# A long convolution by a two-step Fourier transform: the layout of the spectrum between step one and step two

## The chip, the cores and the metric

One core of a Trainium2 chip runs the whole kernel. The metric is device time in microseconds, the median of the runs made; lower is better. The core has a matrix engine (TensorE, in the profile PE for matmuls and PEld for weight loads), VectorE (DVE), ScalarE (ACT), GpSimd (POOL) and SyncE (SP), which issues most DMAs.

## The reference: what is computed

A block with two branches, all in float32, on 2048 tokens by 640 channels. The first branch is a long causal convolution by channel (an H3 mixer), gated by the normalized input; the second a token-mixing MLP. Cut to what matters here:

```python
h = layernorm(x) * (1 + ca) + sa                  # ca, sa, ga from silu(c) @ w_mod
kv = short_conv4(k, shift_k) * v                  # four taps, causal, by channel
y = irfft(rfft(pad(kv)) * rfft(pad(ssm_k)))[:S]   # by channel, length 2 S = 4096
x = x + ga * h * (y + kv * ssm_D)
x = x + gb * mlp_over_tokens(layernorm(x) * (1 + cb) + sb)
```

The change lies in the transform `rfft` of `kv` and of `ssm_k`.

## The kernel before, in words

The five blocks of 128 channels are handled one after another (`c` = 0 to 4, the loop at L510). A block's transform is done on TensorE with float32 matmuls. Time is written as 64 by 32, time = 32 n1 + n2, frequency as 64 k1 by 32 k2.

**Step one** (`step1(side, t)`, L210 to L222) sums over n1. `side` 0 is `kv`, from the tile X, whose channel pairs are read as weights with a step of 32 words; `side` 1 is the filter `ssm_k`, brought into order by `perm` in the tile P and read as contiguous weights. One call takes eight channel pairs (`a` = 0 to 7, pair i = 8 t + a); four calls make a side. For each pair two matmuls, of the cosines and of the sines (`ri`), write 128 columns each, the 64 values of k1 for either channel half, to 64 partitions of a PSUM tile of 1024 words. The columns of one matmul lie side by side; even pairs go to the tile's first bank and odd ones to the second. One ScalarE instruction (L220) then copies the 1024 words to the spectrum Z in SBUF. It reads PSUM in order and writes words at a step of two, so that two neighbouring pairs stand side by side for each k1.

**Step two** (`f2(g)`, L224 to L252) sums over n2. A group g has eight values of k1; for each of them, for the real and the imaginary part and for both channel halves h, a matmul with 64 columns reads all 64 channel columns of its k1 from Z (32 of each side). In Z they lie as 32 pairs of words, 256 words apart. The two halves write different partitions of PSUM. The product of both spectra follows: ScalarE copies the filter's part (L238, tile kt), VectorE multiplies twice (`mul`, L243 and L245, tile p), and POOL, or VectorE for the last group, adds or subtracts into Y (`add`, L251). Every operation of this kind stands in the profile under L59, where the helper TT is.

**The inverse** is `i2` (L263, from Y; ScalarE's copies at L271 write T2, which shares its place with side one of Z) and `i1` (L282, which reads T2 as pairs of words 128 words apart). `gate` multiplies and adds the result into the residual x.

The order of the work is written by hand. For a block c above 0: eight groups of step two, with VectorE's short convolution for the next block (`kv_ops`, its results go to X) mixed in by `dv`; then step one of side 0 for the next block, t = 0 and 1; `i2(0)`; step one t = 2; `i2(1)`; t = 3; `i1(0)`; step one of side 1, t = 0; `i1(1)`; t = 1 to 3. So step two of a block follows the copy of its last tile of side 1. PSUM tiles are taken in turn from a ring of three (`psum`, L69), so a tile of step two can be written again once the VectorE products of the group three before it have read it. In block 4 the fill is layer statistics (`x1s`, L509) and there is no next step one; a few matmuls for the modulation (`mod_part`, L342) stand in its place. After the five blocks come the second norm and the token MLP (L432, L1026, and L951 with seven products in place of eight), which the change doesn't touch.

Constants come ready from the host: F1 (the cosines and sines of step one, 128 columns each, made by `_constants` from `f1`), W2 for step two, V1 and V2 for the inverse.

Of the kernel before, what the change touches and what calls it, by code (L numbers as in the profile page):

```python
# [11 lines left out]
AF = mybir.ActivationFunctionType  # L12
# [8 lines left out]
def _constants():  # L21


    n1, n2, k1, k2 = np.arange(64), np.arange(32), np.arange(64), np.arange(32)
    a = 2 * np.pi * ((1 + 4 * k1)[None, :] * n1[:, None] % 256) / 256
    f1 = np.zeros((2, 64, 2, 2, 64))
    for h in range(2):
        f1[h, :, 0, h], f1[h, :, 1, h] = np.cos(a), np.sin(a)
    ang = 2 * np.pi * ((1 + 4 * k1)[None, :, None] * n2[:, None, None] / 8192
                       + (k2[None, None, :] * n2[:, None, None] % 32) / 32)  # L30
    w2 = np.zeros((2, 32, 2, 64, 2, 2, 32))
    for c in range(2):
        w2[0, :, c, :, 0, c] = np.cos(ang)
        w2[1, :, c, :, 0, c] = -np.sin(ang)
        w2[0, :, c, :, 1, c] = np.sin(ang)
        w2[1, :, c, :, 1, c] = np.cos(ang)
    ang = 2 * np.pi * (k2[:, None] * n2[None, :] % 32) / 32
    c, s = np.cos(ang), np.sin(ang)
    v2 = np.tile(np.concatenate([c, -s, s, c], 1), (4, 1))
    ang = 2 * np.pi * ((1 + 4 * k1)[:, None, None] * (32 * n1[None, None, :] + n2[None, :, None]) % 8192) / 8192  # L40
    v1 = np.tile(np.stack([np.cos(ang), np.sin(ang)], 1).reshape(64, 4096) / 2048, (2, 1))
    sel = np.zeros((128, 128))
    sel[0, 0:64] = sel[1, 64:128] = 1
    small = np.concatenate([f1.reshape(128, 256), v2, np.eye(128)[:, 0:36], sel], 1)
    return {"small": small.astype(np.float32), "w2": w2.reshape(128, 8192).astype(np.float32),
            "v1": v1.astype(np.float32)}
# [3 lines left out]
def mixer_kernel(ctx: ExitStack, tc: tile.TileContext, q, k, v, shift_k, ssm_k, ssm_D, w1, b1, w2, b2, c,  # L50
# [7 lines left out]
    act, dve, pool, pe, sync = nc.scalar, nc.vector, nc.gpsimd, nc.tensor, nc.sync  # L58
# [3 lines left out]
    def mem(tag, n, name=None):  # L62

        return sb.tile([128, n], F32, name=name or tag, tag=tag, bufs=1)
# [4 lines left out]
    def psum(slot=None):  # L69

        uid[0] += 1
        slot = ring[uid[0] % len(ring)] if slot is None else slot
        return psp.tile([128, 1024], F32, name=f"pst_{uid[0]}", tag=f"pst{slot}", bufs=1)
# [6 lines left out]
    T_z, T_y, T_v1 = mem("z", 8192), mem("y", 4096), mem("v", 4520)  # L80
# [11 lines left out]
    KT = [T_kt[:, 512 * i:512 * i + 512] for i in range(2)]  # L92
    TV = T_kt[:, 1024:1536].rearrange("p (n i) -> p n i", i=64)

    Z = T_z.rearrange("p (s t a k e) -> p s t a k e", s=2, t=4, a=8, e=2)
    T2 = T_z[:, 4096:8192].rearrange("p (a m e) -> p a m e", a=32, e=2)
    Y = T_y.rearrange("p (r i k) -> p r i k", r=2, i=32)
    W2 = [t.rearrange("p (k m) -> p k m", m=64) for t in T_w2]
# [2 lines left out]
    F1, V2, ID = SM[:, 0:256], SM[:, 256:384], SM[:, 384:420]  # L101
# [108 lines left out]
    def step1(side, t, later=False):  # L210

        ps = psum()
        for a in range(8):
            i = 8 * t + a
            lhs = KSP[:, i] if side else X.rearrange("p (m i) -> p i m", i=32)[:, i]
            o = 512 * (a % 2) + 128 * (a // 2)
            for ri in range(2):
                pe.matmul(ps[64 * ri:64 * ri + 64, o:o + 128], lhs, F1[:, 128 * ri:128 * ri + 128], start=True,  # L218
                          stop=True)
        evac = lambda: act.activation(Z[:, side, t].rearrange("p a k e -> p e a k"),  # L220
                                      ps.rearrange("p (e a k) -> p e a k", a=8, e=2), AF.Copy)
        return evac if later else evac()  # L222

    def f2(g):  # L224

        ps = psum()
        for kk in range(8):
            k1 = 8 * g + kk
            for ri in range(2):
                for h in range(2):  # L230
                    o = 128 * kk + 64 * ri
                    rhs = bass.AP(tensor=T_z.tensor, offset=T_z.offset + 128 * h + 2 * k1,
                                  ap=[T_z.ap[0], [256, 32], [1, 2]])
                    pe.matmul(ps[64 * h:64 * h + 64, o:o + 64], W2[k1 // 32][:, 2 * (k1 % 32) + ri], rhs, start=True, stop=True)  # L234
        pv = ps.rearrange("p (m s i) -> p m s i", s=2, i=32)
        xs_ = pv[:, :, 0]
        kt = KT[g % 2]
        act.activation(kt.rearrange("p (m i) -> p m i", i=32), pv[:, :, 1], AF.Copy)  # L238
        pa, pb = P[:, 1024 * (g % 2):1024 * (g % 2) + 512], P[:, 1024 * (g % 2) + 512:1024 * (g % 2) + 1024]
        m16 = lambda t: t.rearrange("p (m i) -> p m i", i=32)  # L240

        def mul():
            TT(dve, m16(pa), xs_, m16(kt), ALU.mult)  # L243
            sw = bass.AP(tensor=kt.tensor, offset=kt.offset + 32, ap=[kt.ap[0], [64, 8], [-32, 2], [1, 32]])
            TT(dve, pb.rearrange("p (k r i) -> p k r i", k=8, r=2), xs_.rearrange("p (k r) i -> p k r i", r=2), sw,  # L245
               ALU.mult)

        def add(eng=pool):
            for ri, t, op in ((0, pa, ALU.subtract), (1, pb, ALU.add)):
                t = t.rearrange("p (k r i) -> p r k i", k=8, r=2)  # L250
                TT(eng, Y[:, ri, :, 8 * g:8 * g + 8].rearrange("p i k -> p k i"), t[:, 0], t[:, 1], op)  # L251
        return mul, add  # L252
# [20 lines left out]
    def i1(half, slot=None):  # L273

        ps = psum(slot)
        for jj in range(8):
            for ri in range(2):
                for e in range(2):
                    p = slice(64 * e, 64 * e + 64)
                    for b in range(2):  # L280
                        n2 = 16 * b + 8 * half + jj
                        pe.matmul(ps[64 * b:64 * b + 64, 512 * e + 64 * jj:512 * e + 64 * jj + 64],  # L282
                                  V1[p, ri, n2], T2[p, :, 32 * ri + n2], start=ri == 0, stop=ri == 1)
        return ps
# [200 lines left out]
    for t in range(4):  # L485
        step1(0, t)
# [3 lines left out]
    for t in range(4):  # L490
        step1(1, t)
# [18 lines left out]
    for c in range(NC):  # L510
# [3 lines left out]
        for g in range(8):  # L514
            m_, a_ = f2(g)
            if pend_m:
                pend_m()
            if pend_a:
                pend_a()
            pend_a, pend_m = (pend_m and pa_next), m_  # L520
            pa_next = a_
            if c:
                for f_ in ac[2 * g:2 * g + 2]:
                    f_()
            if cn is None and g < 4:

                act.activation(X[:, 512 * g:512 * g + 1], epsc, AF.Copy)
                for b in range(2):
                    sync.dma_start(X[64 * b:64 * b + 64, 512 * g:512 * g + 512],
                                   dram(w1, (16 * b + g) * F, [[32 * F, 64], [1, 512]]))  # L530
            dv(-(-len(fill) // max((6 if c else 8) - g, 1)))
            if c and cn is not None and g == 3:
                perm_add(cn)
# [13 lines left out]
        if c == 0:  # L547
            mod_load(0, 4, P[:, 0:1920])
            for t in range(4):
                step1(0, t)  # L550
            ps = psum()
# [45 lines left out]
        else:  # L597
# [6 lines left out]
            t = mem("in", 4288, "wb3")  # L604
# [4 lines left out]
        if c:  # L609
            dv(7 if cn is not None else 8)  # L610
            i2(0)
            if cn is None:
                mod_part(tap, 3, pl[3])
                i2(1, dve)
                t = mem("y", 4096, "wb2")
# [19 lines left out]
        for half in range(2):  # L635
            ps = i1(half)
# [37 lines left out]
    start = []  # L674
# [84 lines left out]
    ps = i1(1, s1)  # L759
# [121 lines left out]
    for f_ in range(4, NF):  # L881
        ps = psum().rearrange("p (h m) -> p h m", h=2)
# [123 lines left out]
    for s in range(NW):  # L1006
# [15 lines left out]
        for f_ in range(NF):  # L1022
            u = U[f_]
            for k, (w, r) in enumerate(((wh, 0), (wh, 2), (wl, 0))):
                for h in range(2):
                    pe.matmul(acc[s][:, h, 0:320], w[:, f_].bitcast(F32R), u[r + h].bitcast(F32R),  # L1026
                              start=f_ == 0 and k == 0, stop=f_ == NF - 1 and k == 2)
# [29 lines left out]
def build(inputs):  # L1057
    import concourse.bacc as bacc

    nc = bacc.Bacc("TRN2", target_bir_lowering=False, num_devices=1)  # L1060
    arrays, args = {}, []

    def add(name, a):
        a = np.ascontiguousarray(a)
        arrays[f"in_{name}_dram"] = a
        args.append(nc.dram_tensor(f"in_{name}_dram", a.shape, mybir.dt.from_np(a.dtype), kind="ExternalInput").ap())

    for name in _INS:
        a = np.asarray(inputs[name])
        add(name, a.reshape(S, D) if name in ('A_q', 'A_k', 'A_v') else a)  # L1070
    for name, a in _constants().items():
        add("const_" + name, a)
    args.append(nc.dram_tensor("out_0_dram", (S, D), F32, kind="ExternalOutput").ap())
    with tile.TileContext(nc) as tc:
        mixer_kernel(tc, *args)
    return nc, arrays
# [8 lines left out]
```

## Time and profile before

| what | before |
|---|---|
| median of 3 runs | 719.09 us (716.91 to 719.27) |
| profiled execution, own time | 718.91 us |
| its span, first to last instruction | 716.8 us |
| granted TensorE clock, mean | 0.985 |
| step two, matmul records (L234) | 2560, mean 240 ns, 95.7 us busy |
| step one, matmul records, side 0 / side 1 (L218) | 640 / 640, mean 298 / 281 ns, 44.8 / 39.4 us busy |
| ScalarE's copy after step one (L220) | 40, mean 1140 ns, 45.6 us busy |
| ScalarE's copy after step two (L238) | 40, mean 628 ns, 25.1 us busy |
| VectorE's products (tile p) | 80, mean 685 ns, 51.4 us busy |

Busy time is the time in which at least one instruction of the group ran; matmuls overlap each other, so their mean durations add up to more than the busy time. Each float32 matmul of the source leaves two matmul records and two records of weight loads: 16 matmuls of a call of step one are 32 records, 32 of a group of step two 64. The chain is the line of work that ended last, followed back from release to release; what isn't on it has slack.

### The profile page before, as it was taken

Reading aid. Unit: us, or ns where it says so; the run is one execution under the profiler, and the core shown is the slowest. Engines: PE = TensorE matmul, PEld = TensorE weight load, DVE = VectorE, ACT = ScalarE, POOL = GpSimd, SP = SyncE. Lnnn points to the kernel's source line nnn. Section 1 sums busy time; section 2 is a strip of 40 time slices with the busy share of each in tenths; the row PEclk is TensorE's granted clock in tenths of the full one; section 3 lists DMA queues with packets and bytes.
Section 4 is the critical chain, followed back from the end, with each engine's and each line's share of the span. In section 5 each row is a group of like instructions: output and inputs, shape, how many; then the busy total and the mean of one; then the engine's idle time right before and its main releaser. Section 6 shows DMA issues by size and latency. Waiting matters only on the chain.

```text
span 716.8 us, 20779 instructions
## 1 busy us (share of the span) xinstructions
PE 646.4 (90%) x9131; PEld 624.4 (87%) x9131; DVE 487.0 (68%) x861; ACT 296.9 (41%) x465; POOL 118.4 (17%) x135
## 2 busy tenths in 40 slices
PE   0699677989999989988799999999999989999997
PEld 0699457989999979777799999999999989999997
DVE  7768448969879538888885223112489778888887
ACT  0534373645745636456666223113244222333231
POOL 5183028414324126000110000000000000000000
PEclk9999999999999999999999999999999999999999
DMA  9978988527243522361203633443253523455510
GB/s 184 242 222 229 387 150 165 131 47 158 54 84 90 169 62 63 112 149 31 59 1 59 118 60 60 91 86 59 75 169 104 152 89 122 129 167 168 157 48 37
DMA packets 167184, 84.90 MB, mean 118 GB/s; under 512 B 89235, under 2 KB 157622, under 8 KB 167094
## 3 DMA queue, kind: packets, MB, share of 16 engines
q1 hardware_dynamic: 162546, 82.27, 45.5%
q10 hardware_dynamic: 4548, 1.31, 1.1%
q8 instruction: 71, 1.16, 0.7%
q14 instruction: 19, 0.16, 0.1%
HBM read 73.07 MB, written 10.49 MB: 117 GB/s over the span
## 4 chain that ended last, share of the span: by engine, by line
PE 54%; DVE 22%; DMA 8%; ACT 5%; SPq 5%; issue 4%; POOL 0%; ACTq 0%; DVEq 0%
PE pst L432 21%; PE pst L234 9%; PE pst L218 8%; PE pst L1026 7%; PE pst L263 4%; DVE m_w L59 4%; SPq L495 3%; DVE m_x L59 3%; PE pst L282 2%; DMA aux<-in_A_ssm_k_dram 2%; ACT m_w L939 2%; PE pst L951 2%; DMA aux<-in_w_mod_dram 2%; DVE m_x L960 1%; DVE m_v L59 1%
## 5 line engine op out<-in xcount | busy, mean ns | idle before, releaser
L234 PEld LDWEIGHTS pst<-z,w 128*64 128x64 f32 x2560 | 94.7, 141 | 7.7 <-ACT z L220 7.3
L234 PE MATMUL pst<-z,w 128*64 128x64 f32 x2560 | 95.7, 240 | 6.2 <-ACT z L220 6.1
L218 PE MATMUL pst<-v,x 128*64 128x128 f32 x640 | 44.8, 298 | 24.1 <-DVE x L59 24.0
L220 ACT ACTIVATE z<-pst 128x1024 f32<-128x1024 f32 x40 | 45.6, 1140 | 49.3 <-PE pst L218 30.2
L59 DVE TENSOR_TENSOR p<-pst,kt 128x512 f32<-128x512 f32 x80 | 51.4, 685 | 21.2 <-ACT kt L238 13.4
L218 PEld LDWEIGHTS pst<-v,x 128*64 128x64 f32 x640 | 42.8, 221 | 24.8 <-POOL t L457 23.4
L59 POOL TENSOR_TENSOR y<-p 128x256 f32<-128x256 f32 x72 | 55.2, 800 | 43.4 <-DVE p L59 43.3
L238 ACT ACTIVATE kt<-pst 128x512 f32<-128x512 f32 x40 | 25.1, 628 | 52.6 <-PE pst L234 31.9
L830 ACT ACTIVATE pst<-pst,sm 128x640 f32<-128x640 f32 x14 | 10.7, 767 | 86.0 <-PE pst L432 85.9
L951 PE MATMUL pst<-r_z,m_w 128*128 128x320 f32 x222 | 43.1, 313 | 3.0 <-DVE m_w L59 2.5
L218 PE MATMUL pst<-v,p 128*64 128x128 f32 x640 | 39.4, 281 | 6.5 <-DVE aux L59 4.6
L218 PEld LDWEIGHTS pst<-v,p 128*64 128x64 f32 x640 | 36.8, 141 | 7.8 <-DVE aux L59 4.8
L263 PEld LDWEIGHTS pst<-v,y 32*128 32x128 f32 x1280 | 37.7, 187 | 3.1 <-issue 1.6
L939 ACT ACTIVATE m_w<-m_v 128x896 fp32r<-128x896 f32 x24 | 22.1, 948 | 42.8 <-DVE m_v L59 31.0
L263 PE MATMUL pst<-v,y 32*128 32x64 f32 x1280 | 39.2, 272 | 0.6 <-ACT z L220 0.6
L951 PEld LDWEIGHTS pst<-r_z,m_w 128*128 128x128 f32 x222 | 34.8, 188 | 4.9 <-DVE m_w L59 4.0
L59 DVE TENSOR_TENSOR tap<-tap,kt 128x512 f32<-128x512 f32 x51 | 35.5, 696 | 1.3
L59 DVE TENSOR_TENSOR kt<-in,tap 128x512 f32<-128x512 f32 x51 | 35.0, 686 | 1.4
L59 DVE TENSOR_TENSOR m_w<-m_v,m_w 128x896 fp32r<-128x896 f32 x24 | 26.0, 1087 | 10.5 <-ACT m_w L939 10.5
L282 PEld LDWEIGHTS pst<-z,v 64*64 64x64 f32 x1280 | 24.8, 158 | 7.6 <-issue 4.3
L282 PE MATMUL pst<-z,v 64*64 64x64 f32 x1280 | 26.5, 244 | 5.2 <-issue 2.9
L939 ACT ACTIVATE m_w<-m_p 128x896 fp32r<-128x896 f32 x12 | 11.4, 952 | 47.1 <-DVE m_p L59 40.7
(277 smaller groups left out, 1421.0 us busy)
## 6 DMA issues: line engine op xcount, KB each, us to landing
x<-in_B_w_dram SPq DMA_DIRECT2D x22, 512.0 KB
m_v<-in_B_w_dram SPq DMA_DIRECT2D x15, 384.0 KB
x<-in_B_w_dram SPq DMA_DIRECT2D x14, 384.0 KB
aux<-in_A_ssm_k_dram SPq DMA_DIRECT2D x10, 512.0 KB
in<-in_A_k_dram SPq DMA_DIRECT2D x36, 128.0 KB
in<-in_A_v_dram SPq DMA_DIRECT2D x36, 128.0 KB
m_x<-xs SPq DMA_DIRECT2D x28, 160.0 KB
out_dram<-m_x SPq DMA_DIRECT2D x28, 160.0 KB
```

The lines of the kernel that those rows point to most:

```text
L59: TT = lambda eng, o, a, b, op: eng.tensor_tensor(o, a, b, op=op)
L218: pe.matmul(ps[64 * ri:64 * ri + 64, o:o + 128], lhs, F1[:, 128 * ri:128 * ri + 128], start=True, stop=True)
L220: evac = lambda: act.activation(Z[:, side, t].rearrange("p a k e -> p e a k"), ps.rearrange("p (e a k) -> p e a k", a=8, e=2), AF.Copy)
L234: pe.matmul(ps[64 * h:64 * h + 64, o:o + 64], W2[k1 // 32][:, 2 * (k1 % 32) + ri], rhs, start=True, stop=True)
L238: act.activation(kt.rearrange("p (m i) -> p m i", i=32), pv[:, :, 1], AF.Copy)
L263: pe.matmul(pp[qd // 2][:, o:o + 64], Y[p, ri, i:i + 2].rearrange("p i k -> p (i k)"), V2[p, 64 * ri:64 * ri + 64], start=ri == 0, stop=ri ...
L282: pe.matmul(ps[64 * b:64 * b + 64, 512 * e + 64 * jj:512 * e + 64 * jj + 64], V1[p, ri, n2], T2[p, :, 32 * ri + n2], start=ri == 0, stop=r ...
L432: pe.matmul(ps[0:m, h, 0:320], w_.bitcast(F32R), r_[:, 320 * h:320 * h + 320].bitcast(F32R), start=first and i == 0, stop=last and i == 2)
L495: sync.dma_start(XH[j // 8][64 * b:64 * b + 64, j % 8], dram(q, (16 * b + j) * D, [[32 * D, 64], [1, D]]))
L939: act.activation(W[n][0].bitcast(F32R), a(w_), AF.Copy)
L951: pe.matmul(bank[n], w[:, i].bitcast(F32R), r.bitcast(F32R), start=i == 0 and k == 0, stop=i == 6 and k == 2)
L1026: pe.matmul(acc[s][:, h, 0:320], w[:, f_].bitcast(F32R), u[r + h].bitcast(F32R), start=f_ == 0 and k == 0, stop=f_ == NF - 1 and k == 2)
```

## The change

The layout of the spectrum changes, and with it the three places that write or read it.

- The constant F1 has its columns in another order: k1 outside, channel half inside. Its size and its load are the same.
- Step one's matmuls write their 128 columns with a step of two words. Pair a starts at word 256 (a // 2) + a % 2 of the PSUM tile, so that two neighbouring pairs share a stretch of 256 words, one in the even and one in the odd words. Pairs 0 to 3 are in the tile's first bank, 4 to 7 in the second.
- ScalarE reads the PSUM tile in order as before, and writes two adjacent words at a time, 32 words after the two before (128 times, four times over). Z now has, for each side, one row of 32 words, the channel pairs i, for each k1 and half.
- Step two reads for each k1 and half two runs of 32 words, one of each side, 4096 words apart.

The number of instructions, their sizes, their order and the waits written in the source stay as they are.

```diff
-    f1 = np.zeros((2, 64, 2, 2, 64))
+    f1 = np.zeros((2, 64, 2, 64, 2))
     for h in range(2):
-        f1[h, :, 0, h], f1[h, :, 1, h] = np.cos(a), np.sin(a)
+        f1[h, :, 0, :, h], f1[h, :, 1, :, h] = np.cos(a), np.sin(a)
...
-    Z = T_z.rearrange("p (s t a k e) -> p s t a k e", s=2, t=4, a=8, e=2)
+    Z = T_z.rearrange("p (s k t a e) -> p s t a k e", s=2, k=128, t=4, e=2)
...
-            o = 512 * (a % 2) + 128 * (a // 2)
+            o = 256 * (a // 2) + a % 2
             for ri in range(2):
-                pe.matmul(ps[64 * ri:64 * ri + 64, o:o + 128], lhs, F1[:, 128 * ri:128 * ri + 128], start=True,
+                pe.matmul(ps[64 * ri:64 * ri + 64, o:o + 255:2], lhs, F1[:, 128 * ri:128 * ri + 128], start=True,
                           stop=True)
-        evac = lambda: act.activation(Z[:, side, t].rearrange("p a k e -> p e a k"),
-                                      ps.rearrange("p (e a k) -> p e a k", a=8, e=2), AF.Copy)
+        evac = lambda: act.activation(Z[:, side, t], ps.rearrange("p (a k e) -> p a k e", a=4, e=2), AF.Copy)
...
-                    rhs = bass.AP(tensor=T_z.tensor, offset=T_z.offset + 128 * h + 2 * k1,
-                                  ap=[T_z.ap[0], [256, 32], [1, 2]])
+                    rhs = bass.AP(tensor=T_z.tensor, offset=T_z.offset + 64 * k1 + 32 * h,
+                                  ap=[T_z.ap[0], [4096, 2], [1, 32]])
```

## The prediction

> **What bounds the kernel now.** I read the page first, its engine table and its chain of work.
>
> ```profile
> span 716.8 us, 20779 instructions
> ...
> PE 646.4 (90%) x9131; PEld 624.4 (87%) x9131; DVE 487.0 (68%) x861; ACT 296.9 (41%) x465; POOL 118.4 (17%) x135
> ...
> PE 54%; DVE 22%; DMA 8%; ACT 5%; SPq 5%; issue 4%; POOL 0%; ACTq 0%; DVEq 0%
> PE pst L432 21%; PE pst L234 9%; PE pst L218 8%; PE pst L1026 7%; PE pst L263 4%; DVE m_w L59 4%; SPq L495 3%; DVE m_x L59 3%; PE pst L282 2%; DMA aux<-in_A_ssm_k_dram 2%; ACT m_w L939 2%; PE pst L951 2%; DMA aux<-in_w_mod_dram 2%; DVE m_x L960 1%; DVE m_v L59 1%
> ```
>
> TensorE carries 54% of the chain. The two steps that the diff touches, step two (L234) and step one (L218), hold 9% and 8% of it, some 65 and 54 us; everything after 300 us (L432, L1026, L951) is untouched and only starts earlier or later. So the second view is the chain in order of time, from 117 to 300 us (columns: start, length, what).
>
> ```profile
> 132.11 5.09 PE pst L234 x128
> ...
> 168.53 19.03 PE pst L234 x507
> 187.55 4.12 PE pst L218 x64
> 191.67 3.73 PE pst L263 x128
> 195.40 2.28 PE pst L218 x30
> ...
> 201.60 2.24 PE pst L218 x32
> ...
> 205.87 2.06 PE pst L218 x32
> 207.93 2.18 PE pst L282 x128
> 210.11 5.42 PE pst L218 x96
> ...
> 215.60 1.09 ACT z L220
> 216.74 19.05 PE pst L234 x495
> ...
> 266.82 19.09 PE pst L234 x508
> 285.90 3.36 PE tap L342 x36
> 289.26 3.73 PE pst L263 x128
> ...
> 385.58 141.07 PE pst L432 x960
> ```
>
> The reader is to see that in the channel blocks 2, 3 and 4 step two stands whole on the chain, 19 us at a stretch; in block 1 only its last 5.09 us do, because VectorE leads before. Block 0's step two, from 41 us on, is not on the chain: the issue of the q loads and DMAs are. Step one stands on the chain with all its 256 records of a block, and ScalarE's copy (L220) with one instruction, the last before step two.
>
> **Part one, step two reads runs of 32 words.** The third view is TensorE's timeline, which gives the spacing of matmuls; the fourth the single lines (durations: least, median, most).
>
> ```profile
> 216.74 19.05 PE L234 MATMUL pst<-z,w 128*64 128x64 f32 x512 [1.24 <-ACT z L220]
> 207.86 2.25 PE L282 MATMUL pst<-z,v 64*64 64x64 f32 x128
> 203.77 2.10 PE L282 MATMUL pst<-z,v 64*64 64x64 f32 x128
> 187.45 4.22 PE L218 MATMUL pst<-v,x 128*64 128x128 f32 x63
> 210.04 5.46 PE L218 MATMUL pst<-v,p 128*64 128x128 f32 x96
> ```
> ```profile
> L234 PE MATMUL pst<-z,w x2560: 222/240/282, 41.1 to 285.7; 128*64 128x64 f32 x197
> L282 PE MATMUL pst<-z,v x1280: 212/216/367, 94.9 to 309.9; 64*64 64x64 f32 x183
> L218 PEld LDWEIGHTS pst<-v,x x640: 186/222/240, 23.4 to 252.0; 128*64 128x64 f32 x160
> L218 PEld LDWEIGHTS pst<-v,p x640: 132/137/230, 32.6 to 265.2; 128*64 128x64 f32 x160
> L218 PE MATMUL pst<-v,p x640: 272/273/421, 32.8 to 265.3; 128*64 128x128 f32 x160
> ```
>
> Each matmul of the source leaves two records (an 8 x 2 x 2 loop, 64 records a group). The two halves of L234 run beside each other, so a record of one half follows the last one every 2 x (19.05 - 0.24)/511 = 73.6 ns, for 64 columns. Two rows say that 64 columns can go faster. L218 with contiguous weights and a contiguous moving operand takes 2 x (5.46 - 0.27)/95 = 109 ns for 128 columns, so half of it, 55 ns, is the lower end. L282, also 64 columns, runs four records beside each other, one round every 4 x (2.10 - 0.22)/127 = 59 ns. And L234's median lasts 240 ns against 216 in L282: its stream is some 20 ns slow. Weights are no reason for it: L234 loads 64 contiguous words, as L218 on "p", where loads hide under 109 ns. What is left as different is the reading: pairs 256 words apart, both halves 128 words from each other. L282 reads pairs too, but 128 words apart and its two streams 32 words apart. After the change step two reads two runs of 32 words. I take 59 ns, of the row with the same 64 columns; 55 and 73.6 (no gain) are the ends.
>
> [...]
>
> A group of step two then takes 32 x 59 = 1.89 us instead of 2.38, a block 15.2 instead of 19.05. Whether the rest keeps up is VectorE's question: a group may write its PSUM tile only when the products (line 243) of the group three before have read it, and the inverse (L263) needs the last sums. VectorE's timeline:
>
> ```profile
> 220.63 1.28 DVE L59 TENSOR_TENSOR p<-pst,kt 128x512 f32<-128x512 f32 x2
> 221.82 0.69 DVE L59 TENSOR_TENSOR tap<-tap,kt 128x512 f32<-128x512 f32 x1
> 222.55 0.69 DVE L59 TENSOR_TENSOR kt<-in,tap 128x512 f32<-128x512 f32 x1
> ...
> 229.61 1.29 DVE L59 TENSOR_TENSOR p<-pst,kt 128x512 f32<-128x512 f32 x2 [0.42 <-POOL y L59]
> 237.80 1.08 DVE L59 TENSOR_TENSOR y<-p 128x256 f32<-128x256 f32 x2
> ...
> 133.21 1.28 DVE L59 TENSOR_TENSOR p<-pst,kt 128x512 f32<-128x512 f32 x2
> 282.41 1.27 DVE L59 TENSOR_TENSOR p<-pst,kt 128x512 f32<-128x512 f32 x2
> 286.71 1.29 DVE L59 TENSOR_TENSOR p<-pst,kt 128x512 f32<-128x512 f32 x2 [0.99 <-POOL y L59]
> ```
>
> *Block 3.* The first products start at 220.63 with or without the change, held by the convolution's operations ahead of them. From there VectorE has 8 pairs of products at 1.2 us (220.63 to 221.82) and 7 fill operations at 0.73 (221.82 to 222.55): back to back the fifth pair of products (now at 229.61) starts at 228.6 and ends at 229.9, so the eighth group runs from 230.0 to 231.9, and TensorE alone would be done at 216.74 + 15.2 = 231.9 as well. The sums end at 235.3 instead of 238.9; 4.1 us of step one lie between, so L263 starts at 236.0, not 239.9. Gain 3.85 us. *Block 2* is built alike: 3.85. *Block 4*: statistics fill VectorE until the sixth product at 282.41; only the 0.5 us by which the first copy is early pass through. The last two then follow directly: products at 283.1 and 284.3, sums until 286.6, so L263 starts at 286.7 instead of 289.26: 2.5. *Block 1*: VectorE leads; the eighth group waits for the fifth product (133.21, 0.5 earlier by the earlier first copy), runs from 134.0 to 135.9 instead of ending at 137.2: 1.3. *Block 0*: off the chain, nothing; what comes before 110 us waits for SyncE and DMAs. Sum: 3.85 + 3.85 + 2.5 + 1.3 = 11.5 us; with 55 ns, and VectorE as above, some 12, with 64 ns 8. What hides the rest of the work, VectorE's fill and POOL's sums, is then used up: VectorE is late next.
>
> **Part two, ScalarE's copy.** ScalarE reads PSUM in order before and after. It now writes two adjacent words at a step of 32, where it wrote single words at a step of two: both ways two words fall into each sixteen bytes touched.
>
> ```profile
> L220 ACT ACTIVATE z<-pst x40: 1067/1134/1221, 27.0 to 265.7; 128x1024 f32<-128x1024 f32 x40
> L421 ACT ACTIVATE wb0b<-x x14: 937/1047/1058, 379.4 to 544.5; 128x1024 fp32r<-128x1024 f32 x10, 128x896 fp32r<-128x896 f32 x4
> L170 ACT ACTIVATE tap<-rows x3: 657/663/663, 95.3 to 189.0; 128x256 f32<-128x256 f32 x3
> ```
>
> In order, 1024 words take 1047 ns, and 0.86 ns is a word's price (1047 and 937 for 1024 and 896), so 166 are fixed. L170 reads single words 16 bytes apart: (663 - 166)/256 = 1.94 ns each. So the copy lies between 1.05 and 2.15 us; I take 1.13, nothing changed, as L220's own step leaves the same words per sixteen bytes. Its cover is thin: 1.0 us more would be paid once a block ahead of step two (4 x 1.0), and where three copies follow each other every 5.46/3 = 1.8 us (96 records of step one make three tiles), 0.3 each time again: 4 x 1.0 + 12 x 0.3, some 8 us.
>
> **Part three, the step of two in PSUM.** No row shows TensorE writing PSUM with a step. Lower end: nothing, and no gain either, since addresses are all that changes. Upper end: half speed, a column costing as much as two. The stream's price is (273 - 216)/64 = 0.89 ns a column, so 128 columns cost 114 more, taken at 110 with 107 as their time at the spacing's 0.83: side one's pair goes from 109 to 219, side zero's from 2 x (4.22 - 0.29)/62 = 127 (its strided weights load in 222 ns against 137 and set that spacing) to 219. On the chain stand per block 64 pairs of side one and 63 of side zero: 7.0 + 5.8 = 12.8 us, three times, and 3.5 ahead of block 1: 42 us. I take nothing: these matmuls deliver a column in about 0.85 ns, while L432, 960 records in 141 us, delivers 320 columns in 147 ns, 0.46 ns a word, so that PSUM takes nearly two adjacent words in the time that step one needs for one.
>
> [...]
>
> **The sum.** -11.5 + 0 + 0. The profiled execution took 718.9 us (span 716.8), the median is 719.1. Forecast 707.5 us.
>
> **The rivals.**
> *A, as forecast* (0.59): 703 to 712, the bounds of step two's spacing and half a microsecond a block for the copy. For it: the 20 ns that L234 alone loses.
> *B, reading isn't the reason* (0.11): the 73.6 ns come of something that stays, a limit of 128 rows by 64 columns, say. For it: pairs run well in L282. Time 719, within 0.3%.
> *C, PSUM's step is paid* (0.23): step one slows to up to half speed on the chain, 42 - 11.5 = +30: 749 us (761 if B holds too). It decides from where the pair's extra x eats the gain: side one pays on 224 pairs, side zero on 189 with 18 ns spare, 0.224x + 0.189(x - 18) = 11.5, x = 36 ns, a third of half speed. For it: nothing in the trace excludes it. Against it: the slow column rate of these matmuls.
> *D, the copy slows to 2 us* (0.07): -11.5 + 8: 715. Against it: the same two words per sixteen bytes.
>
> **How the numbers follow.** This kernel's runs tell about 0.3% (2.2 us) from no change. Faster: A and D, 0.66; same: B, 0.11; slower: C, 0.23. A alone would reach from 703 to 712, with B and D to 720. More than 2 in 10 would be left out above, so the range takes in C's likeliest value: 702 to 749.
>
> **What would show it.** Step two's stretches on the chain at 15.2 us and L234's median near 216 ns (A), or 19.05 and 240 (B). L218's median on "p" at 273 and its 96 records in 5.4 us (A), or near 380 and 10 (C). L220's median near 1.13 us, or near 2 (D). VectorE between 216 and 236 us without the idle time ahead of its last four products. Wrong would be the whole if step one's spacing grows by more than 36 ns a pair, or if step two gets faster but L263 still starts as late, held by VectorE.

## The result and the profile after

| what | before | after |
|---|---|---|
| median of 5 runs each, side by side | 719.09 us (716.91 to 721.52) | 713.51 us (711.57 to 714.59) |
| ratio, 95% interval | | 0.9923 [0.99, 0.9946] |
| profiled execution, its span | 718.9, 716.8 us | 711.7, 709.6 us |
| granted TensorE clock | 0.985 | 0.969 |

The changed kernel is faster by 5.6 us, about half of the 11.5 us that the prediction worked out. Ratios and their intervals leave out slow executions, of which two medians further below, 702.64 and 707.64 us, hold one each. From L220 on, lines stand one lower than before: step two is L233, the inverse L262 and L281.

The page of the changed kernel, its span, engine table, one DMA queue and chain:

```profile
span 709.6 us, 20770 instructions
...
PE 636.7 (90%) x9131; PEld 612.2 (86%) x9131; DVE 484.7 (68%) x861; ACT 292.5 (41%) x465; POOL 114.0 (16%) x135
...
q8 instruction: 71, 1.16, 0.7%
...
PE 48%; DVE 28%; DMA 8%; ACT 6%; issue 5%; SPq 3%; POOL 1%; ACTq 0%; DVEq 0%; POOLq 0%
```

TensorE's share of the chain fell from 54% to 48%, VectorE's rose from 22% to 28%: work moved over, as forecast. "Issue", time for which the profile shows no cause, is at 5%. The queue q8 carries instructions, 71 packets with 1.16 MB, so 16,384 bytes each; it becomes the main thing below.

The single lines of the changed kernel (durations: least, median, most):

```profile
L233 PE MATMUL pst<-z,w x2560: 216/222/270, 41.7 to 279.1; 128*64 128x64 f32 x197
L218 PE MATMUL pst<-v,p x640: 272/273/474, 33.4 to 260.1; 128*64 128x128 f32 x160
L220 ACT ACTIVATE z<-pst x40: 1025/1064/1114, 27.5 to 260.4; 128x1024 f32<-128x1024 f32 x40
```

Step two's median fell from 240 to 222 ns, step one's stayed at 273 and the copy's went from 1134 to 1064. All three local costs came about as forecast (216, 273 and 1130 ns). But the stretches of step two on the chain are not whole. The chain of the changed kernel in order of time (start, length, what):

```profile
154.26 1.38 issue
155.64 1.53 PE pst L218 x24
...
158.85 1.62 issue
...
221.28 7.77 PE pst L233 x255
229.05 0.93 issue
229.98 0.22 PE pst L233
230.20 4.18 PE pst L218 x64
234.38 1.93 PE pst L262 x61
236.31 0.78 issue
237.09 2.22 PE pst L262 x67
...
275.58 1.88 PE pst L233 x57
277.45 1.46 issue
278.91 0.45 PE pst L233 x7
```

At 229.05 one matmul of step two is left, and TensorE stands still for 0.93 us before it; at 277.45 seven are left, and it stands still for 1.46. The profile shows nothing that holds them there. TensorE's waits between 110 and 290 us show the sums (what waits, for what, us in total, times, longest), first before, then after:

```profile
...
PE pst L282 <- issue: 2.1, 2, 1.3
PE pst L218 <- issue: 1.1, 1, 1.1
```
```profile
...
PE pst L233 <- issue: 3.4, 5, 1.5
PE pst L233 <- DVE p L59: 2.6, 6, 1.2
PE pst L281 <- issue: 1.6, 1, 1.6
PE pst L218 <- issue: 1.4, 1, 1.4
PE pst L262 <- issue: 0.8, 1, 0.8
PE pst L218 <- DVE p L59: 0.4, 1, 0.4
```

Before, step two never waits for "issue"; after, it does so for 3.4 us, beside 2.6 us for VectorE's products. All waits of this kind rose from 3.2 to 7.2 us; with one of 0.11 us, which this view leaves out, they are 7.3.

**What they have in common.** Count TensorE's records of the trace from 0 in order of start, weight loads, matmuls and semaphore instructions alike. Every one of these idle times stands just ahead of a record whose number is 193 above a multiple of 256. The 18,339 records hold 71 such places, and q8 has 71 packets; with 64 more instructions, as tried below, it is 72 of either. So a packet of q8 is taken here for a block of 256 TensorE instructions, 64 bytes each; an idle time at its border is called a late block below, while blocks 1 to 4 are those of 128 channels. All nine idle times of the changed kernel between 110 and 290 us end 1.20 to 1.46 us after the end of a packet. A group of step two has 64 matmul records and 64 weight loads, so step two uses up a block in 3.73 us now, where it took 4.70 before. In the trace of after one border is crossed at 225.10; the next fetch packet starts 2.60 us later, ends at 228.64, and TensorE goes on at 229.98, 1.34 us after that. Likewise the packet that ends at 277.51 is used at 278.91. From the border to the use of the packet that follows it went 4.9 us, more than the 3.73 that a block lasts. In most places of step two a packet ends 1 to 2.7 us after a border, so that by the same 1.3 us it could be used after 2.3 to 4 us: 4.7 us covered that, 3.73 hardly do.

By block, from the first matmul of step two to the first of the inverse (us), with the forecast gain:

| block | before | after | gain | forecast | idle at block borders after |
|---|---|---|---|---|---|
| 1 | 23.81 | 23.20 | 0.6 | 1.3 | 0.19, 0.61 |
| 2 | 23.08 | 20.20 | 2.9 | 3.85 | 0.20 |
| 3 | 23.11 | 20.97 | 2.1 | 3.85 | 0.93 |
| 4 | 22.38 | 21.20 | 1.2 | 2.5 | 1.46 |

Together 6.8 us. Between block 1's inverse and block 2's step two 1.0 is lost (the late blocks at 154 and 159 us cost 3.0 where two cost 1.9 before), 0.6 more in the same stretch of blocks 2 and 3; 0.7 is won after block 4 and 1.4 ahead of block 1, where DMAs lead. The profiled pair's difference is 7.2 us.

### The profile page after: what moved, and what is told of

It reads as the page before. It is cut to its first block, busy times and chain, and to the rows that moved or that the text cites. A ratio compares the mean times of both kernels' runs of the same rounds, so it can differ in the third digit from the quotient of the medians.

```text
span 709.6 us, 20770 instructions
## 1 busy us (share of the span) xinstructions
PE 636.7 (90%) x9131; PEld 612.2 (86%) x9131; DVE 484.7 (68%) x861; ACT 292.5 (41%) x465; POOL 114.0 (16%) x135
## 3 DMA queue, kind: packets, MB, share of 16 engines
q8 instruction: 71, 1.16, 0.7%
## 4 chain that ended last, share of the span: by engine, by line
PE 48%; DVE 28%; DMA 8%; ACT 6%; issue 5%; SPq 3%; POOL 1%; ACTq 0%; DVEq 0%; POOLq 0%
PE pst L431 21%; PE pst L218 7%; PE pst L1025 7%; PE pst L262 5%; DVE m_w L59 4%; DVE p L59 3%; PE pst L233 3%; DVE tap L59 3%; DVE m_x L59 3%; DVE kt L59 2%; PE pst L281 2%; DMA in<-in_A_v_dram 2%; PE pst L950 2%; ACT m_w L938 1%; DMA in<-in_A_k_dram 1%
## 5 line engine op out<-in xcount | busy, mean ns | idle before, releaser
L233 PE MATMUL pst<-z,w 128*64 128x64 f32 x2560 | 78.9, 223 | 12.2 <-ACT z L220 5.7
L233 PEld LDWEIGHTS pst<-z,w 128*64 128x64 f32 x2560 | 76.7, 138 | 13.9 <-ACT z L220 6.9
L220 ACT ACTIVATE z<-pst 128x1024 f32<-128x1024 f32 x40 | 42.6, 1065 | 52.2 <-PE pst L218 52.0
L59 POOL TENSOR_TENSOR y<-p 128x256 f32<-128x256 f32 x72 | 51.1, 742 | 36.9 <-DVE p L59 36.7
L262 PEld LDWEIGHTS pst<-v,y 32*128 32x128 f32 x1280 | 37.8, 187 | 4.2 <-issue 2.8
L262 PE MATMUL pst<-v,y 32*128 32x64 f32 x1280 | 39.5, 272 | 1.4 <-issue 0.8
L270 ACT ACTIVATE z<-pst 128x512 f32<-128x512 f32 x38 | 21.3, 656 | 21.2 <-PE pst L262 21.2
L281 PEld LDWEIGHTS pst<-z,v 64*64 64x64 f32 x1280 | 23.8, 154 | 7.1 <-issue 3.2
```

Of the source, the lines that this page charges most:

```text
L59: TT = lambda eng, o, a, b, op: eng.tensor_tensor(o, a, b, op=op)
L220: evac = lambda: act.activation(Z[:, side, t], ps.rearrange("p (a k e) -> p a k e", a=4, e=2), AF.Copy)
L262: pe.matmul(pp[qd // 2][:, o:o + 64], Y[p, ri, i:i + 2].rearrange("p i k -> p (i k)"), V2[p, 64 * ri:64 * ri + 64], start=ri == 0, stop=ri ...
L270: act.activation(o, i, AF.Copy)
```

## Experiments: the three parts of the change

Theory one: step one's PSUM step costs nothing, the copy's cost hangs on how many adjacent words it writes, and the gain is step two's. The rivals: PSUM's step or the copy gives part of it back.

**PSUM's step alone**, with the spectrum and step two as before:

```diff
-            o = 512 * (a % 2) + 128 * (a // 2)
+            o = 256 * (a // 2) + a % 2
-                pe.matmul(ps[64 * ri:64 * ri + 64, o:o + 128], lhs, ...
+                pe.matmul(ps[64 * ri:64 * ri + 64, o:o + 255:2], lhs, ...
-        evac = lambda: act.activation(Z[:, side, t].rearrange("p a k e -> p e a k"), ...
+        evac = lambda: act.activation(T_z[:, 4096 * side + 1024 * t:4096 * side + 1024 * t + 1024], ps, AF.Copy)
```

> Only PSUM's step of two: step one writes every second word, F1 keeps its old column order, so that PSUM holds the old spectrum's order and ScalarE copies 1024 words in order; step two reads pairs 256 words apart as before. Theory one (the step is free; half of the forecast gain was lost elsewhere): step one's median on p stays at 273 ns, its 96 records at 5.4 us, step two's stretches stay at 19.05 us, the copy falls to 1.05 us, and the time to 4 x 0.08 = 0.3 us below the kernel before, ratio 0.999 to 1.000. Rival (the step costs something and has eaten 6 us of the forecast 11.5): some 5.6 us slower than the kernel before, ratio 1.008.

Measured: 718.59 us, ratio 0.9989 [0.9962, 1.0015]. Its single lines:

```profile
L218 PE MATMUL pst<-v,p x640: 272/273/475, 34.0 to 264.4; 128*64 128x128 f32 x160
L220 ACT ACTIVATE z<-pst x40: 1001/1024/1042, 27.2 to 264.8; 128x1024 f32<-128x1024 f32 x40
L233 PE MATMUL pst<-z,w x2560: 221/240/283, 42.3 to 284.7; 128*64 128x64 f32 x197
```

Step one lasts 273 ns with and without the step: rival C falls. The copy in order takes 1024 ns, step two without its new reading stays at 240. By itself the PSUM step neither gains nor costs, within this interval.

**The new spectrum from a contiguous PSUM tile**, so that ScalarE has to write single words 32 apart:

```diff
-                pe.matmul(ps[64 * ri:64 * ri + 64, o:o + 255:2], lhs, ...
+                pe.matmul(ps[64 * ri:64 * ri + 64, o:o + 128], lhs, ...
-        evac = lambda: act.activation(Z[:, side, t], ps.rearrange("p (a k e) -> p a k e", a=4, e=2), AF.Copy)
+        evac = lambda: act.activation(Z[:, side, t].rearrange("p a k e -> p e a k"),
+                                      ps.rearrange("p (e a k) -> p e a k", a=4, e=2), AF.Copy)
```

> The new spectrum without PSUM's step: step one writes columns side by side as before, ScalarE reads them in order and writes single words 32 apart, step two reads runs of 32 words. Theory one (a copy of one word per sixteen bytes costs 1.94 ns a word, as L170 before): the copy takes about 2.1 us, step two's groups 1.87 us; on the chain 1.0 us a block ahead of step two and 0.3 for three copies each, so 4 to 8 us above the changed kernel, 718 to 722 us. Rival (words 32 apart cost ScalarE no more than pairs): copy 1.07 us, time 713.5 us.

Measured: 716.37 us, ratio 0.998 [0.9939, 1.002]. Its single line of the copy:

```profile
L220 ACT ACTIVATE z<-pst x40: 1900/1959/2092, 26.9 to 264.3; 128x1024 f32<-128x1024 f32 x40
```

Single words cost 1959 ns, pairs 1064. Most of the gain is gone, about 4 us of it by the two ratios, the least of the 4 to 8 us expected; the interval is wide. This is what PSUM's step is good for: it lets ScalarE write pairs.

**Which property of the reading makes step two slow?** Both kernels read pairs of the old spectrum that don't belong together; the work is the same, and only their times count. First pairs 128 words apart with the halves in different sides, then pairs 256 apart, as before, with the halves 32 words from each other instead of 128:

```diff
-                    rhs = bass.AP(..., offset=T_z.offset + 128 * h + 2 * k1, ap=[T_z.ap[0], [256, 32], [1, 2]])
+                    rhs = bass.AP(..., offset=T_z.offset + 4096 * h + 2 * k1, ap=[T_z.ap[0], [128, 32], [1, 2]])
```

> The kernel before, but step two reads its 32 pairs 128 words apart instead of 256, one half's stream in each side of the spectrum (words that do not belong to it, so the result is another; the work is the same). Theory (256 words between pairs, or the two halves 128 words from each other, slow the reading): spacing of a pair of records 59 ns, groups 1.9 us. Rival (64 columns over 128 rows with pairs are slow whatever the distance): 73.6 ns, groups 2.4 us.

```diff
-                    rhs = bass.AP(..., offset=T_z.offset + 128 * h + 2 * k1, ap=[T_z.ap[0], [256, 32], [1, 2]])
+                    rhs = bass.AP(..., offset=T_z.offset + 32 * h + 2 * k1, ap=[T_z.ap[0], [256, 32], [1, 2]])
```

> The kernel before, but the two halves of step two read pairs 32 words from each other instead of 128, the pairs still 256 apart (words that do not belong to it, so the result is another). Theory (the two streams meet in the same place of the memory): 59 ns, groups 1.9 us. Rival (the 256 words between pairs of one stream slow it): 73.6 ns, groups 2.4 us.

That execution fell to a granted clock of 0.753 (795.27 us) and can't be compared; the same kernel again:

> The kernel before, with step two's two halves reading pairs 32 words from each other in place of 128, once more, since the first such run went at a granted clock of 0.753. Theory (the two streams meet in the same place of the memory when 128 or 4096 words lie between them; with 128 words between pairs and halves 4096 apart the spacing was still 70 to 73 ns): 58 to 59 ns a pair of records, groups 1.87 us, at a clock near 0.98. Rival (pairs as such are slow over 128 rows): 73 ns.

Measured: 714.58 us for the first, 713.65 for the second, one execution each. Their single lines of step two, the first kernel's first:

```profile
L234 PE MATMUL pst<-z,w x2560: 216/240/281, 39.7 to 281.7; 128*64 128x64 f32 x197
```
```profile
L234 PE MATMUL pst<-z,w x2560: 216/219/273, 41.4 to 280.5; 128*64 128x64 f32 x197
```

For the first the faster reading had been expected, and it did not come: with pairs 128 words apart and 4096 words between the halves the median is still 240. What counts here is how far the streams of the two halves, which run at the same time, lie from each other: with the pairs 256 words apart in both, 128 words between the halves cost 240 ns and 32 words 219. So pairs as such are not slow. Why 32 words between the streams are fast and 128 are not, no run here shows.

## Experiments: where the other half of the gain is

Two theories. One: VectorE is late and holds step two's PSUM tiles. The other: TensorE's own instructions come late, as blocks of 256 fetched over a queue.

**Relieve VectorE**, on both kernels: the short convolution covers one eighth of its rows (7/8 of it is left out).

```diff
-    def kv_ops(g, eng=dve):
+    def kv_ops(g, eng=dve, n=8):
-        w = lambda s: W_[:, None, s, :].to_broadcast([128, 8, 64])
+        w = lambda s: W_[:, None, s, :].to_broadcast([128, n, 64])
...
-            o = kv_ops(gl[0])
+            o = kv_ops(gl[0], n=1)
```

> The changed kernel with VectorE relieved: the short convolution that is mixed into the blocks' loop works on one of eight time rows (7/8 of it left out), same number of instructions, about 0.2 us each in place of 0.7. Theory one (VectorE's order holds back step two's groups): the gain over the equally relieved kernel before grows from 5.6 to 10 us or more, since groups follow each other at 1.87 us and VectorE is never late. Theory two (TensorE's instructions come too late: 256 of them last 3.73 us in step two now, 4.67 before, and the idle times without a releaser stand at every 256th record): the gain stays near 6 us, and the idle times at every 256th record grow, since nothing else holds TensorE.

> The kernel before with the same relief of VectorE (7/8 of the short convolution in the blocks' loop left out): the base that the relieved changed kernel is compared with. Both theories: step two's stretches stay at 19.05 us in blocks 2 to 4 and fall from 19.6 to 19.05 in block 1; little time at every 256th record inside step two.

Measured: 705.08 us, 0.9847 [0.9788, 0.9906], with the change; 716.56, 0.9978 [0.995, 1.0006], without. Between them lie 11.5 us, by the two intervals 4.7 more or less, as theory one expected. Theory two, near 6 us and more idle time at the borders, is a miss: the idle time fell from 7.3 to 5.1 us. In TensorE's timeline of the relieved changed kernel, block 3's step two:

```profile
206.05 15.15 PE L234 MATMUL pst<-z,w 128*64 128x64 f32 x512 [1.12 <-ACT z L221]
```

512 records in 15.15 us, 2 x 14.9/511 = 58 ns a pair, where 59 was forecast. By blocks the gains are 2.4, 3.2, 4.0 and 0.9 us. Block 1, where VectorE leads, gains 1.8 more than without the relief. In block 3 the late block of 0.93 us is gone from step two, though TensorE's program is the same, and in block 4 one still takes 1.73 us. So both causes are at work, and this pair of runs does not part them; that its 11.5 us equal the forecast, which counted VectorE with all its work, is chance.

**Leave the loads out**, on both: the DMAs that bring the next blocks' k, v and filter while the blocks run (those of the weights remain).

```diff
-                if c_next is not None:
+                if False:
...
-        if c and c + 2 < NC:
-            load_ks(c + 2)
```

> The changed kernel without the loads of k, v and the filter that the loop issues for later blocks (stale values are used, so the result is another). Theory two (the instruction packets wait behind these loads): the idle times at every 256th record of TensorE between 110 and 290 us, 7 us in the changed kernel, fall under 2 us, and it gains 3 to 5 us over the changed kernel. Rival (the packets' delay has nothing to do with the loads): idle times and time stay within 1 us.

> The kernel before without the same loads. Theory two: it had 3.2 us of such idle time between 110 and 290 us, none inside step two, and gains 1 to 3 us, less than the changed kernel does; the gain of the change without these loads is 7 to 9 us in place of 5.6. Rival: the gain of the change stays at 5.6 us.

Measured: 709.85 us, 0.9898 [0.9846, 0.9951], and 716.6, 0.9984 [0.9955, 1.0013]. Without these loads the change is worth (0.9984 - 0.9898) x 717.9 = 6.2 us, where 7 to 9 were expected, and the idle times at borders fell from 7.3 to 4.8 us only, where under 2 were expected: both are misses. Those near 125, 155 and 160 us, beside the loads left out, went from 0.61, 1.38 and 1.62 to 0.29, 0.71 and 0.25; those near 229, 236 and 278 us stayed at 0.92, 0.73 and 1.73, where the weights' loads go on. But the changed kernel run again (below) has 0.22, 0.77 and 1.07 us at the first three places with all its loads, and in the kernel before the idle times did not fall without them (3.2 and 3.5 us). So this pair of runs does not show that the loads delay the fetch.

The traces of the two kernels say more. Take each border between 110 and 290 us and the share of the 16 DMA engines' time that the packets of the other queues fill in the 1.5 us after it. In the changed kernel the fetch starts 0.86 us after the border (median of 18) where that share is under 0.3, and 1.66 us after it (median of 15) where it is over 0.7; in the kernel before it is 0.38 us (21) and 1.71 us (10). The fetches behind the idle times near 229, 236 and 278 us start 2.6, 4.9 and 4.0 us after their borders, at shares of 0.7 to 1.0. So a late fetch goes with busy DMA engines; a run that changes their traffic alone at these borders was not made.

**Move the borders.** If blocks are the cause, extra TensorE instructions at the start move every later border to another place of the program. Sixteen idle matmuls of 64 x 64 words are 64 instructions; 32 are 128.

```diff
+    dummy = psum(0)
+    uid[0] -= 1
+    for i in range(16):
+        pe.matmul(dummy[0:64, 0:64], ones, ones, start=True, stop=True)
```

> The changed kernel with 16 more small matmuls (64 TensorE instructions) at the start, while TensorE waits for the first loads. Theory (instructions are fetched in blocks of 256, and one that comes late stops TensorE): the idle times without a releaser again stand at record 193 of every 256 counted from the start, so 64 instructions earlier in the program; none stays at the last record of step two of blocks 3 and 4, where 0.93 and 1.46 us stood. Rival (these places wait for something of their own): the idle times stay at the same instructions of the program. The time moves by less than 4 us either way.

> The same with 32 small matmuls (128 instructions). Theory: idle times at record 193 of every 256, 128 instructions earlier in the program than in the changed kernel. Rival: at the same instructions as there. The time moves by less than 4 us either way.

> The changed kernel with 16 small matmuls at the start once more, with more runs: 702.6 us came of four runs that lay between 698 and 710. Theory (its blocks arrive in time; only VectorE's order holds it): 702 to 704 us, ratio 0.977 to 0.981, no more than 1.5 us of idle time at record 193 of every 256 between 110 and 290 us. Rival (a lucky run; blocks come late by chance at any place): 706 us or more.

> The changed kernel with 24 small matmuls (96 instructions) at the start, between the two shifts already run. Theory (the place of the block borders decides and neighbouring places are alike): between them, 702 to 706 us. Rival (each run draws its delays anew): 708 us or more.

> The changed kernel itself, on the chip of the three others, for the comparison: 713.5 us, ratio 0.992 to the kernel before.

| kernel | us | ratio to the kernel before | idle at borders, 110 to 290 us |
|---|---|---|---|
| changed | 713.51 | 0.9923 [0.99, 0.9946] | 7.3 |
| changed, again | 711.94 | 0.9913 [0.9885, 0.9941] | 7.5 |
| changed, 64 more | 702.64 | 0.9768 [0.9713, 0.9823] | 0.9 |
| changed, 64 more, again | 703.41 | 0.9806 [0.9774, 0.9839] | 0.3 |
| changed, 96 more | 703.44 | 0.9807 [0.9774, 0.9841] | 1.1 |
| changed, 128 more | 705.04 | 0.9825 [0.9789, 0.986] | 2.0 |

Matmuls that compute nothing win 6 to 11 us, by the ratios, where less than 4 us either way had been expected. The granted clock is not the reason: with 96 more it was 0.961 to 0.968, in the changed kernel run again 0.968 to 0.988. The idle times that are left still stand at records 193 of 256, thus 64 instructions earlier in the program. The chain with 64 more instructions, second run, in order of time:

```profile
171.29 7.68 PE pst L233 x256
178.97 4.08 PE pst L218 x64
183.05 3.73 PE pst L262 x128
...
215.66 7.68 PE pst L233 x256
223.34 4.08 PE pst L218 x64
227.42 3.73 PE pst L262 x128
```

and its waits of TensorE between 110 and 290 us:

```profile
PE pst L233 <- ACT z L220: 4.6, 4, 1.2
PE pst L233 <- DVE p L59: 3.6, 7, 1.2
...
PE pst L218 <- DVE p L59: 0.4, 1, 0.4
PE pst L281 <- issue: 0.3, 1, 0.3
```

Step two, step one and the inverse follow each other without a gap. Ahead of each block step two waits for ScalarE's last copy, and within it for VectorE alone, as the prediction had it. The blocks take 23.25, 19.64, 19.64 and 19.44 us. This version is faster than both kernels.

**The same shift on the kernel before**, as the control:

> The kernel before with the same 16 small matmuls at the start. Theory (a block of 256 instructions lasts 4.67 us in its step two, so that a late block seldom stops it, and the shift is worth little without the change): within 3 us of the kernel before, ratio 0.996 to 1.003, so that the change is worth 11 us or more at this place of the blocks. Rival (the shift is a gain of its own, whatever step two does): 8 us or more below the kernel before, and the change is worth 5 to 7 us at any place.

> The kernel before with 32 small matmuls at the start. Theory: within 3 us of the kernel before. Rival: 8 us or more below it.

Measured: 714.3 us, 0.995 [0.9926, 0.9975], and 714.46, 0.9968 [0.9943, 0.9994]; its idle times at borders went from 3.2 to 0.4 and 1.7. So the kernel before wins 2 to 4 us by it, at 64 a little more than the 3 expected and far from the rival's 8, the changed one more than twice that. With borders in the same place the change is worth (0.995 - 0.9806) x 717.5 = 10.3 us at 64, and (0.9968 - 0.9825) x 717.5 = 10.3 us at 128, each 3 us more or less by the intervals, where 11 or more had been expected; the first of the two runs at 64 would make it 13.1. By blocks at 64: 23.83, 23.07, 23.08 and 22.36 before, so gains of 0.6, 3.4, 3.4 and 2.9, together 10.4.

**Give POOL a quarter of the short convolution** for blocks 3 and 4, so that VectorE is free earlier; without a shift and with 64 more instructions:

```diff
...
-                fill.extend(kv(c + 3 if c + 3 < NC else None))
+                *first_, last_ = kv_ops(2, pool)
+                run(first_)
+                fill.extend(kv(c + 3 if c + 3 < NC else None, ((0,), (1, 2), (3,))))
...
+            if c + 2 < NC:
+                last_()
...
-            dv(11 if c else 8)
+            dv(9 if c else 8)
```

> The changed kernel with a quarter of the short convolution of the blocks 3 and 4 (the group of time rows 16 to 23) done on POOL, which idles 19 us a block, and not on VectorE; two of VectorE's fill operations move from before step two into it. Theory one (VectorE's order holds back step two): from the start of step two to the start of the inverse 20.2 and 21.0 us in blocks 2 and 3 fall to about 19.3, some 2.5 us in all, 711 us, ratio to the kernel before 0.988. Rival (POOL's work slows VectorE's, or TensorE's late instructions take it): no gain over the changed kernel, ratio 0.992 or more.

> The changed kernel with 16 small matmuls at the start and a quarter of the short convolution of blocks 3 and 4 on POOL. Theory (both hold back what the change gives: late instructions and VectorE): from the start of step two to the inverse 19.2 us in blocks 2 and 3 in place of 20.0 and 19.7, so about 1 us below the kernel with the shift alone, 701.5 us. Rival (POOL's part is worth nothing): within 0.3% of it or above.

Measured: 711.15 us, 0.9908 [0.9877, 0.9939], and 707.64, 0.9855 [0.9817, 0.9893], where 701.5 was expected: a miss, and slower than the shift alone. For the first 0.988 was expected, at the end of its interval; it is no better than the changed kernel (0.9913), which was the rival's outcome. In the first, block 2 takes 19.28 us as expected and block 3 21.44, with late blocks of 0.25 and 1.15 us in it (the profile puts the second down to ScalarE's copy, but it stands at a border, 1.6 us after its packet's end). In the second, TensorE's timeline of block 3:

```profile
211.50 6.80 PE L233 MATMUL pst<-z,w 128*64 128x64 f32 x225 [1.14 <-ACT z L220]
...
219.43 3.95 PE L233 MATMUL pst<-z,w 128*64 128x64 f32 x127 [1.13 <-issue]
225.60 6.37 PE L233 MATMUL pst<-z,w 128*64 128x64 f32 x159 [2.22 <-issue]
```

The late blocks are back, 1.13 and 2.22 us in one step two. TensorE's program is the one of the shift alone, so the borders stand at the same instructions; what changed is when the packets came, 2.7 and 3.8 us after their borders here, 0.5 and 0.2 us there. So the place of a border does not decide alone. A shift is no cure but luck, and a change elsewhere can undo it.

## Why the prediction was right and wrong

**Step two's price: right.** 59 ns a pair was taken, from L282; 58 to 59 came (15.15 us for 512 records, 7.68 for 256). The reason given (the reading) held, in the form that the distance of the two streams counts (240 ns a record at 128 words, 219 at 32, the pairs 256 apart in both), not that pairs are 256 words apart. B fell.

**PSUM's step: right.** 273 ns both ways. C fell, and with it the upper half of the range. Half speed, from which the 42 us and the 749 come, was the author's assumption; no run shows it, and with the step side one's median stayed at 273 ns in both runs that have it (the changed kernel and the step alone).

**The copy: right.** 1.064 us against 1.13; D's 2 us is the price of single words (1.959 us 32 apart), which the change avoids. That D's 715 us lies near the measured time is chance, and so is it that 713.5 lies between 702 and 749: A's own range ended at 712, and the rest above was there for C, which fell.

**VectorE: right.** In VectorE's timeline of the changed kernel, block 3's fifth pair of products:

```profile
225.23 1.27 DVE L59 TENSOR_TENSOR p<-pst,kt 128x512 f32<-128x512 f32 x2
```

It ends at 226.50, 13.2 us after step two's start at 213.34; forecast was 229.9 - 216.74 = 13.2.

**The step that failed** is "A group of step two then takes 32 x 59 = 1.89 us instead of 2.38, a block 15.2 instead of 19.05", together with "VectorE is late next". The sum asked of VectorE and ScalarE whether they keep up, and not of TensorE's own supply of instructions, whose delay it put at nothing without a reason. The runs showed 7.3 us of it in place of 3.2 before. In blocks 3 and 4 a late block stood in step two (0.93 and 1.46 us); the two ahead of block 2, there before too, grew by 1.1. With the borders moved in both kernels, 10.3 us of the forecast 11.5 are there, 3 us more or less. Of the rest, 0.7 us is block 1, where 0.6 came of 1.3; blocks 2 and 3 are 0.4 short each, and block 4 gained 0.4 more than forecast. In block 1 step one's first tile takes the PSUM place of step two's sixth group and waits for its products until 135.07 us, when step two had ended at 134.78; the prediction counted that wait for step two alone.

**Could the profile have told it?** The trace of before has such idle times, 3.2 us in three places, called "issue", and the count of 256 could have been read from them. In step two, at 4.7 us a block, the supply kept up with little to spare at the tightest border: the packet ended 2.95 us after it, so that by the 1.3 us above it could be used after some 4.3.

**Left open:** why a packet starts late (in the changed kernel from 2.0 us before to 4.9 us after its border; 34 of the 37 between 110 and 290 us start after it, and each ends at least 1.2 us before the next border is crossed). It goes with busy DMA engines, by the shares above, but the runs without loads did not bear this out, and the weights' loads were not tried apart.

## What to carry to other kernels

When TensorE is made faster, ask how long a block of 256 of its instructions lasts (weight loads count: the 32 float32 matmuls of a group of step two left 64 matmul records and 64 of weight loads): in this kernel step two stood still at some borders when a block lasted 3.73 us and at none when it lasted 4.70, and idle time called "issue" at a record 193 above a multiple of 256 was its mark. Where a change wins less than its parts, run both kernels with some more TensorE instructions at the start before blaming a part, since 64 to 128 of them alone moved these kernels by 2 to 11 us. Place streams that run at the same time by trial: moving two of them from 128 to 32 words apart made step two as fast (219 ns a record in place of 240) as runs of 32 words did (222).

## What the runs showed of the hardware that was not expected

- TensorE stood still for up to 2.22 us at a border of 256 (POOL's part with 64 more, block 3), where step two uses up a block in 3.73 us; the nine idle times of the changed kernel ended 1.20 to 1.46 us after the end of a packet of q8.
- A packet of q8 started 0.86 us after its border where the other DMA queues filled under 0.3 of the engines' time, 1.66 us where they filled over 0.7 (medians of 18 and 15, the changed kernel).
- Two float32 streams of 64 columns beside each other: 240 ns a record when 128 or 4096 words apart, 219 when 32 apart, each as pairs of words.
- ScalarE writing 1024 words to SBUF: 1024 ns in order, 1064 as pairs 32 apart, 1134 at a step of two, 1959 as single words 32 apart.
- A step of two words in PSUM costs these 128-column float32 matmuls nothing (273 ns both ways).
